# Six places for the copies on their way to DRAM, a cast moved behind the stores, two sums moved past a marker

## The chip, the cores and the metric

The kernel runs on one core of a Trainium2 chip. The metric is the device time of one execution in microseconds (us), the median over runs. A core has a matrix engine (PE, with its weight loads listed as PEld), a vector engine (DVE), a scalar engine (ACT), a general engine (POOL) and a queue engine (SP); SP, POOL and ACT also issue DMA transfers, and 16 DMA engines carry them.

## The reference, cut to what matters

Attention with a sigmoid in place of the softmax, then a feed-forward block with a GELU, all in float32:

```python
# q, k, v: (8, 12, 448, 64); w_in: (768, 2048); w_out: (2048, 768)
scores = scale * np.matmul(q, k.transpose(0, 1, 3, 2)) - np.log(S)
attn = 1.0 / (1.0 + np.exp(-scores))
attn_out = np.matmul(attn, v)                     # (8, 12, 448, 64)
x = attn_out.transpose(0, 2, 1, 3).reshape(3584, 768)
h = x @ w_in
g = 0.5 * h * (1.0 + erf(h * inv_sqrt2))
return g @ w_out
```

## The kernel before, in words

**Two stages.** The attention runs first (0 to 256 us of the trace), then the feed-forward block (256 us to the end, 4032 matmuls without a pause). The attention is cut into 24 **units** of four heads, three units for each of the eight batches. Units 0, 1 and 18 to 23 run alone (`single`); units 2 to 17 run two at a time (`paired`, on u = 2, 4, ..., 16; "pair u" below is units u and u + 1). The order on every engine is the order in which the code is written; there is no scheduler.

**A pair on PE.** Twelve score tiles (L482, each three times two matmuls, 72 in all, since each operand is split into `hi` and `lo`), then the values of unit u in two halves (L518) with a small score tail between them (L502), then the values of unit u + 1 in the same way. Four places in PSUM, named by `perm`, hold score tiles and the products `pav` of the values in turn. The fourth score tile of the next pair takes the place in which `pav` of unit u + 1 lies, so it can start only when that has been copied out.

**Marker.** Between the halves of `values`, DVE copies two columns of `pav` into `mark` (L545, the tile `ones` in the profile). PE starts the second half only after that copy, so whatever stands ahead of it on DVE can hold up PE.

**Out of PSUM.** `park(u, p)` is called twice for a unit, at the end of its values: DVE copies half p of `pav` (448 columns) into a place in SBUF (L572) and POOL issues the store from there to the DRAM tensor `scr_x` (L573). The places come from `piece` (tag `tmp`), a ring of three, so that each copy waits until the store of three copies earlier has landed. For the first two batches (u below 6) the copies go mostly straight to SBUF tiles that stay there.

**Casts and differences.** `high_qk` rounds a loaded q/k tile to `hi`, on POOL or DVE (L439), and `split_qk` lets DVE take `lo` = raw - `hi` (L448). In pair u POOL casts three tiles for the next pair: halves 0 and 1 of unit u + 2 and half 0 of unit u + 3 (`after`; pair 16 has only the first two). Half 1 of unit u + 3, the fourth, is cast by DVE during the next scores.

**Decoder.** Meanwhile the two weight matrices are decoded in steps: `go(3)` gives DVE the operations L179, L187 and L194, and `post` lets it take four sums (L107 to L110) and POOL issue seven stores to `scr_in` (L213). In pair u this is: `go(3)` ahead of the first values, `post` between their halves (`idle1`), `go(3)` between the second values' halves (`idle2`). `STEPS` gives the steps of units 18 to 23: how many ahead of the values, how many behind the marker.

**Queues.** Each engine works strictly in order. POOL's row in a pair of before is: three casts, seven stores of the decoder, two stores of unit u, two stores of unit u + 1.

Of the kernel before, what the change touches and what calls it, by code (L numbers as in the profile page):

```python
# [8 lines left out]
F32 = mybir.dt.float32  # L9
# [6 lines left out]
ALU = mybir.AluOpType  # L16
# [6 lines left out]
def tile_sigmoid_attention_gelu_ffn(  # L23
# [10 lines left out]
    nc = tc.nc  # L34
    B, NPAIR, _, S = q.shape
    NU = NPAIR // 2
    D = HALF
    NF, _, NC, _ = w_in.shape
    NO, _, NFH, _ = w_out.shape
# [4 lines left out]
    HT = S // 2  # L44
# [71 lines left out]
    def piece(name):  # L116
        return sb.tile([P, S], F32, tag="tmp", name=name, bufs=3)
# [162 lines left out]

    dec = Decoder()
    PAIRED = range(2, 18, 2)
    STEPS = {18: (3, 0), 20: (3, 1), 21: (4, 1), 22: (4, 1), 23: (4, 0)}
    wst_all = sb.tile([P, WST * WU], F32, name="wst_all", bufs=1)
    STEPS_IN_ALL = 5 * len(CHUNKS) + 2

# [64 lines left out]
    def rows(j):  # L351
        return slice(j * D, j * D + D)

    def x_tile(tag, name):
        pool, bufs = (sb, 4) if tag == "xs" else (late, 1)
        return pool.tile([P, KC, S], F32R, tag=tag, name=name, bufs=bufs)
# [25 lines left out]
    x0 = {(j, k): x_tile("xs", f"x0_{j}{k}") for j, k in ((1, 0), (0, 0), (0, 1), (1, 1))}  # L382
    h0 = sb.tile([P, KC, S], F32R, tag="h0", name="xh0_p1", bufs=1)
    x6 = sb.tile([P, KC, S], F32, tag="h1", name="x0_p6", bufs=1)

    def attention(at, ps):
        raws, vals, parts, probs, pavs = {}, {}, {}, {}, {}
        total = B * NU
        SINGLE = PAIRED[-1] + 2
# [15 lines left out]
        def vacate(u, p, c):  # L405
            vacant.append(probs.pop((u, p, c)))

        def load(u):
            if u >= total or u in loaded:
                return  # L410
            loaded.add(u)
            b, n = divmod(u, NU)
            raw = at.tile([P, 2, 2, S], F32, tag="qk", name=f"qk{u}", bufs=3)
            for pp in (slice(0, 1), slice(1, 2)) if u == 0 else (slice(0, 2),):
                if u == 0 and pp.start == 1:
                    nc.scalar.activation(one, one, AF.Sigmoid)
                hps = slice(2 * n + pp.start, 2 * n + pp.stop)
                nc.sync.dma_start(raw[:, pp, 0], q[b, hps].rearrange("p r s -> r p s"))
                for j in range(2):
                    src = k[b, hps, rows(j), j].rearrange("p r s -> r p s")  # L420
                    queue = nc.scalar if j == 0 and u == 0 else nc.sync
                    queue.dma_start(raw[rows(j), pp, 1], src)  # L422
            raws[u] = raw

        def load_v(u):
            if u >= total:
                return
            b, n = divmod(u, NU)
            vr = at.tile([P, 2, 2, FULL + 1, D], F32, tag="v", name=f"v{u}", bufs=3)
            for p in range(2):  # L430
                nc.sync.dma_start(vr[:, p], v[b, 2 * n + p])
            vals[u] = vr

        def high_qk(u, p, copy):
            hi, lo = (
                at.tile([P, 2, S], F32R, tag=x, name=f"{x}{u}_{p}", bufs=3) for x in ("hi", "lo")
            )
            parts[u, p] = hi, lo
            copy(hi, raws[u][:, p])  # L439

        def split_qk(u, p):
            if u >= total:
                return
            raw = raws[u][:, p]
            if (u, p) not in parts:
                high_qk(u, p, nc.vector.tensor_copy)
            hi, lo = parts[u, p]
            nc.vector.tensor_tensor(lo, raw, hi, op=ALU.subtract)  # L448
# [62 lines left out]
        def values(u, i, tail, order, meanwhile, idle):  # L511
# [39 lines left out]
            for p in range(2):  # L551
                for c in range(FULL):
                    vacate(u, p, c)

        def park(u, p):
            if u < 0:
                return
            b, n = divmod(u, NU)
            if b < 2:
                j, c = divmod(2 * n + p, KC)  # L560
                for i in range(2):
                    dst = x0[j, i].bitcast(F32)[:, c, b * HT : b * HT + HT]
                    src = pavs[u][:, p, i * HT : i * HT + HT]
                    if (j, i) == (0, 0):
                        x = piece(f"x{u}_{p}")[:, :HT]
                        nc.vector.tensor_copy(x, src)
                        nc.gpsimd.dma_start(dst, x)
                    else:
                        nc.vector.tensor_copy(dst, src)
                return  # L570
            x = piece(f"x{u}_{p}")
            nc.vector.tensor_copy(x, pavs[u][:, p])  # L572
            nc.gpsimd.dma_start(scr_x[:, 2 * n + p, b * S : (b + 1) * S], x)  # L573

        def decode(u, place):
            if u >= total:
                return
            if u == total - 1:
                dec.second = first_sum
            dec.go(STEPS.get(u, (0, 0))[place])  # L580

# [12 lines left out]
        def single(u):  # L594
            for p in range(2):
                for c in range(FULL):
                    scores(u, p, c, perm[(FULL * p + c) % 4])
            if u == 0:
                scores_tail(u, perm[3])
            load(u + 3)  # L600
            if u > 0:
                split_qk(u + 1, 0)
                split_qk(u + 1, 1)
            decode(u, 0)
            if u == SINGLE + 1:
                x01, x11, x00 = (x0[jk].bitcast(F32) for jk in ((0, 1), (1, 1), (0, 0)))
                nc.vector.tensor_tensor(x01, x11, x01, op=ALU.subtract)
                nc.vector.tensor_tensor(x6, x01, x00, op=ALU.add)
            if u == SINGLE + 2:
                lo = x0[0, 0]  # L610
                nc.vector.tensor_tensor(lo, lo.bitcast(F32), h0, op=ALU.subtract)

            def meanwhile():
                if u == 0:
                    split_qk(1, 0)
                    split_qk(1, 1)
                if u + 1 == PAIRED[0]:
                    split_qk(u + 2, 0)
                decode(u, 1)
                if u == total - 1:  # L620
                    W.low_to(3)

            def idle():
                if u == SINGLE + 1:
                    nc.scalar.copy(h0, x0[0, 0].bitcast(F32))
                if u >= total - 4:
                    W.high_to(W.ready + 1)

            order = [0, 1, 2, FULL] if u == 0 else [FULL, 0, 1, 2]
            values(u, perm[2], perm[3], order, meanwhile, idle)  # L630
            for p in range(2):
                park(u, p)
            if u in (total - 3, total - 2):
                W.low_to(u - total + 4)
            load_v(u + 2)
            if u == 0:
                dec.go(1)
            if u in (total - 6, total - 5):
                W.load_to(2 * (u - total + 7))

        def paired(u):
            a, b, c, d = perm
            begun = u > PAIRED[0]
            after = [(u + 2, 0), (u + 2, 1)]
            if u + 2 < SINGLE:
                after.append((u + 3, 0))
            load(u + 3)
            load_v(u + 2)
            tiles = [(w, p, c) for w in (u, u + 1) for p in range(2) for c in range(FULL)]
            for n, at_tile in enumerate(tiles):  # L650
                if n == FULL:
                    high_qk(u + 1, 1, nc.vector.tensor_copy)
                scores(*at_tile, perm[n % 4], evict if n in (3, 7) else sigmoid)
                if n == 3:
                    split_qk(u + 1, 1)
                if n in (8, 11):
                    late_sigmoid(*tiles[{8: 3, 11: 7}[n]])
            for w, p in after:
                high_qk(w, p, nc.gpsimd.tensor_copy)
            split_qk(*after[0])  # L660
            if begun:
                dec.go(3)

            def idle1():
                load(u + 4)
                dec.post()
                if len(after) > 2:
                    split_qk(*after[2])
                dec.begin_next()

            values(u, a, b, [FULL, 1, 2, 0], lambda: None, idle1)
            for p in range(2):
                park(u, p)
            load_v(u + 3)
            split_qk(*after[1])

            def idle2():
                load(u + 5)
                dec.go(3)
                dec.begin_next()  # L680

            values(u + 1, c, d, [0, 1, 2, FULL], lambda: None, idle2)
            for p in range(2):
                park(u + 1, p)

        u = 0
# [355 lines left out]
```

## Time and profile before

| | |
|---|---|
| median of 3 runs | 1023.78 us (1019.7 to 1024.88) |
| profiled execution, its own time | 1024.35 us |
| its span in the trace | 1022.6 us |
| PE busy | 1007.7 us (99%) |
| DVE busy | 724.9 us (71%) |
| ACT busy | 667.5 us (65%) |
| POOL busy | 128.8 us (13%) |
| mean granted clock of PE | 0.997 of full speed |

The busy shares are means over two very different stages. PE counts as busy until the modelled end of a matmul, so a short wait can hide behind the end of the one before it; the length of a stretch that holds the same work each time tells more. The 1.75 us between span and time lie outside the trace, before the first and behind the last instruction.

### The profile page before, as it was taken

Reading aid. Unit: us, or ns where it says so; the run is one execution under the profiler, and the core shown is the slowest. Engines: PE = TensorE matmul, PEld = TensorE weight load, DVE = VectorE, ACT = ScalarE, POOL = GpSimd, SP = SyncE. Lnnn points to the kernel's source line nnn. Section 1 sums busy time; section 2 is a strip of 40 time slices with the busy share of each in tenths; the row PEclk is TensorE's granted clock in tenths of the full one; section 3 lists DMA queues with packets and bytes.
Section 4 is the critical chain, followed back from the end, with each engine's and each line's share of the span. In section 5 each row is a group of like instructions: output and inputs, shape, how many; then the busy total and the mean of one; then the engine's idle time right before and its main releaser. Section 6 shows DMA issues by size and latency. Waiting matters only on the chain.

```text
span 1022.6 us, 16579 instructions
## 1 busy us (share of the span) xinstructions
PE 1007.7 (99%) x6406; PEld 903.8 (88%) x6406; DVE 724.9 (71%) x842; ACT 667.5 (65%) x920; POOL 128.8 (13%) x191
## 2 busy tenths in 40 slices
PE   9999999999999999999999999999999999999998
PEld 5655555455999999999999999999999999999998
DVE  3687887777997998683368877634887674368873
ACT  5786676678897666566666655666656467666652
POOL 0244434232232120010000000100000000000000
PEclk9999999999999999999999999999999999999999
DMA  9988999897998584565344455644444553434441
GB/s 272 269 272 287 323 346 330 294 347 231 315 338 278 171 273 142 153 190 173 110 136 124 123 151 164 215 123 124 128 118 149 149 162 110 124 98 135 136 139 66
DMA packets 83215, 199.17 MB, mean 195 GB/s; under 512 B 9408, under 2 KB 33984, under 8 KB 83136
## 3 DMA queue, kind: packets, MB, share of 16 engines
q1 hardware_dynamic: 69360, 152.24, 48.7%
q0 software_dynamic: 11840, 39.23, 11.1%
q10 hardware_dynamic: 1936, 6.63, 2.0%
q8 instruction: 51, 0.84, 0.3%
q14 instruction: 28, 0.23, 0.1%
HBM read 156.10 MB, written 41.29 MB: 193 GB/s over the span
## 4 chain that ended last, share of the span: by engine, by line
PE 85%; DMA 8%; DVE 2%; POOL 2%; issue 2%; SPq 0%; POOLq 0%; ACT 0%; DVEq 0%
PE pf L704 75%; PE sc L482 5%; PE pav L518 5%; DMA scr_x<-x 4%; DMA qk<-k_dram 3%; POOL scr_in L213 2%; DMA raw<-w_in_dram 1%; DVE lo L448 1%; PE sc_t L502 1%; PE pav L532 0%; DMA qk<-q_dram 0%; DVE x L572 0%; POOL hi L439 0%; SPq L422 0%; DVE hi L439 0%
## 5 line engine op out<-in xcount | busy, mean ns | idle before, releaser
L704 PE MATMUL pf<-op,whl 128*128 128x448 f32 x2016 | 382.1, 353 | 0.0
L704 PEld LDWEIGHTS pf<-op,whl 128*128 128x128 f32 x2016 | 380.9, 189 | 0.5 <-DVE op L741 0.2
L704 PE MATMUL pf<-xh_p,whl 128*128 128x448 f32 x1296 | 353.0, 353 | 0.0
L338 DVE TENSOR_TENSOR whl<-wst_all,whl 128x768 fp32r<-128x768 f32 x224 | 213.7, 955 | 153.7 <-ACT whl L331 153.3
L331 ACT CAST whl<-wst_all 128x768 fp32r<-128x768 f32 x224 | 186.0, 830 | 142.4 <-PE pf L704 124.5
L704 PEld LDWEIGHTS pf<-xh_p,whl 128*128 128x128 f32 x1296 | 244.9, 189 | 1.4 <-issue 0.7
L704 PE MATMUL pf<-xl_p,whl 128*128 128x448 f32 x624 | 219.9, 352 | 0.0
L741 DVE TENSOR_TENSOR op<-g,op 128x896 fp32r<-128x896 f32 x112 | 121.5, 1086 | 0.9 <-ACT op L751 0.9
L704 PEld LDWEIGHTS pf<-xl_p,whl 128*128 128x128 f32 x624 | 117.9, 189 | 0.1
L751 ACT CAST op<-g 128x896 fp32r<-128x896 f32 x112 | 104.8, 936 | 1.7 <-PE pf L704 1.7
L518 PE MATMUL pav<-a_all,v 64*64 64x448 f32 x936 | 104.4, 541 | 0.7 <-DVE ones L545 0.7
L457 ACT ACTIVATE a_all<-sc 128x896 f32<-128x896 f32 x91 | 77.6, 930 | 26.3 <-PE sc L482 26.3
L518 PEld LDWEIGHTS pav<-a_all,v 64*64 64x64 f32 x936 | 37.5, 132 | 50.0 <-issue 38.5
L741 DVE TENSOR_TENSOR g<-g,g 128x896 f32<-128x896 f32 x64 | 69.5, 1086 | 0.0
L738 ACT ACTIVATE g<-tmp 128x448 f32<-128x448 f32 x64 | 40.3, 631 | 38.2 <-DVE tmp L741 38.1
L482 PE MATMUL sc<-lo,hi 64*128 64x448 f32 x276 | 54.6, 380 | 9.8 <-DVE x L572 9.8
L738 ACT ACTIVATE g<-pf 128x448 f32<-128x448 f32 x64 | 34.8, 543 | 39.8 <-PE pf L704 39.7
L363 POOL DMA_DIRECT2D x<-scr_x x24 | 18.0, 806 | 324.8 <-ACT g L848 204.2
L741 DVE TENSOR_TENSOR tmp<-pf,g 128x448 f32<-128x448 f32 x64 | 39.8, 623 | 26.2 <-PE pf L704 16.6
L448 DVE TENSOR_TENSOR lo<-qk,hi 128x896 fp32r<-128x896 f32 x46 | 53.8, 1170 | 5.9 <-POOL hi L439 5.4
L482 PE MATMUL sc<-hi 64*128 64x448 f32 x276 | 51.8, 359 | 0.0
L482 PE MATMUL sc<-hi,lo 64*128 64x448 f32 x276 | 51.7, 359 | 0.0
(85 smaller groups left out, 925.8 us busy)
## 6 DMA issues: line engine op xcount, KB each, us to landing
wst_all<-scr_in SPq DMA_DIRECT2D x112, 384.0 KB, 3.2
wst_all<-scr_out SPq DMA_DIRECT2D x112, 384.0 KB, 3.2
v<-v_dram SPq DMA_DIRECT2D x48, 256.0 KB, 9.6
raw<-w_in_dram SPq DMA_DIRECT2D x16, 767.8 KB, 9.9
out_dram<-tmp SPq DMA_DIRECT2D x47, 224.0 KB, 2.1
qk<-q_dram SPq DMA_DIRECT2D x23, 448.0 KB, 9.2
qk<-k_dram SPq DMA_DIRECT2D x46, 224.0 KB, 9.8
scr_out<-wd POOLq DMA_DIRECT2D x36, 256.0 KB, 5.1
```

The costliest lines, as they stand in the source:

```text
L213: nc.gpsimd.dma_start(scr_in[n // 2][:, n % 2], parts[p])
L331: nc.scalar.copy(hl[:, 0], t)
L338: nc.vector.tensor_tensor(hl[:, 1], t, hl[:, 0], op=ALU.subtract)
L363: queue.dma_start(dst[:, :, a], src[:, :, a])
L448: nc.vector.tensor_tensor(lo, raw, hi, op=ALU.subtract)
L457: nc.scalar.activation(to, sc, AF.Sigmoid, bias=NEG_LOG_S, scale=SCALE)
L482: nc.tensor.matmul(sc[:, j], ks[rows(j), 1, keys], braid(qs[rows(j), 0]) if braided else qs[rows(j), 0], start=n == 0, stop=n == last,)
L518: nc.tensor.matmul(pav[rows(j), p], vals[u][half, p, j, c], a[p][half, j], start=not swap and c == order[0], stop=c == (order[-1], FULL - ...
L704: nc.tensor.matmul(bank, a, braid(m), **flags)
L738: nc.scalar.activation(straight(dst), unbraid(src), AF.Gelu)
L741: nc.vector.tensor_tensor(out, a, b, op=op)
L751: nc.scalar.copy(op[:, 0], src)
```

## The change

Three things are changed.

1. `parked` gives `park` its place. A number n = 2u + p counts the copies. Below unit 18, n mod 6 of 0 to 2 takes a place of the old ring, n mod 6 of 3 to 5 takes one of the three slices of `x6` (the tile `x_p` in the rows), which holds nothing until unit 19. From unit 18 on it is the ring of three alone.
2. In `paired`, the third tile of `after` (half 0 of unit u + 3) is cast by POOL behind the stores of unit u, no longer ahead of the decoder's seven stores; its `lo` is taken by DVE in `idle2`, behind the second marker and ahead of `go(3)`, no longer in `idle1`.
3. In the last units, the sum into `x6` (unit 19) and the difference into `x0[0, 0]` (unit 20) go behind the marker, and of unit 18's three decoder steps one does.

```diff
-    STEPS = {18: (3, 0), 20: (3, 1), 21: (4, 1), 22: (4, 1), 23: (4, 0)}
+    STEPS = {18: (2, 1), 20: (3, 1), 21: (4, 1), 22: (4, 1), 23: (4, 0)}
...
+        def parked(u, p):
+            n = 2 * u + p
+            if u >= SINGLE or n % 6 < 3:
+                return piece(f"x{u}_{p}")
+            return x6[:, n % 3]
+
         def park(u, p):
...
-                        x = piece(f"x{u}_{p}")[:, :HT]
+                        x = parked(u, p)[:, :HT]
...
-            x = piece(f"x{u}_{p}")
+            x = parked(u, p)
...
             decode(u, 0)
+            x01, x11, x00 = (x0[jk].bitcast(F32) for jk in ((0, 1), (1, 1), (0, 0)))
             if u == SINGLE + 1:
-                x01, x11, x00 = (x0[jk].bitcast(F32) for jk in ((0, 1), (1, 1), (0, 0)))
                 nc.vector.tensor_tensor(x01, x11, x01, op=ALU.subtract)
-                nc.vector.tensor_tensor(x6, x01, x00, op=ALU.add)
-            if u == SINGLE + 2:
-                lo = x0[0, 0]
-                nc.vector.tensor_tensor(lo, lo.bitcast(F32), h0, op=ALU.subtract)
 
             def meanwhile():
+                if u == SINGLE + 1:
+                    nc.vector.tensor_tensor(x6, x01, x00, op=ALU.add)
+                if u == SINGLE + 2:
+                    nc.vector.tensor_tensor(x0[0, 0], x00, h0, op=ALU.subtract)
...
-            for w, p in after:
+            for w, p in after[:2]:
                 high_qk(w, p, nc.gpsimd.tensor_copy)
             split_qk(*after[0])
...
             def idle1():
                 load(u + 4)
                 dec.post()
-                if len(after) > 2:
-                    split_qk(*after[2])
                 dec.begin_next()
...
             load_v(u + 3)
+            for w, p in after[2:]:
+                high_qk(w, p, nc.gpsimd.tensor_copy)
             split_qk(*after[1])
 
             def idle2():
                 load(u + 5)
+                for w, p in after[2:]:
+                    split_qk(w, p)
                 dec.go(3)
                 dec.begin_next()
```

On DVE, in pair 6, from the last of the decoder's sums to the cast of the fourth tile, before (`lo_0_948` is the difference of the third tile, `lo_1_945` that of the second, `x_...<-pav` are the copies of `park`):

```order
L110 TENSOR_TENSOR sin_984<-wd_811,sin_984 128x384
L448 TENSOR_TENSOR lo_0_948<-qk_807,hi_0_947 128x896
L572 COPY x_0_1012<-pav_956 128x448
L572 COPY x_1_1015<-pav_956 128x448
L448 TENSOR_TENSOR lo_1_945<-qk_741,hi_1_944 128x896
L545 COPY ones<-pav_1022 128x2
L179 SCALAR_TENSOR_TENSOR wd_1050<-raw_715,me_997 128x768
L187 TENSOR_SCALAR raw_715<-raw_715 128x768
L194 ISA wd_1050<-raw_715,wd_1050 128x1536
L572 COPY x_0_1071<-pav_1022 128x448
L572 COPY x_1_1074<-pav_1022 128x448
L439 CAST hi_1_1104<-qk_807 128x896
```

The same place after the change:

```order
L110 TENSOR_TENSOR sin_981<-wd_811,sin_981 128x384
L578 COPY x_0_1008<-pav_953 128x448
L578 COPY x_1_1011<-pav_953 128x448
L448 TENSOR_TENSOR lo_1_945<-qk_738,hi_1_944 128x896
L545 COPY ones<-pav_1021 128x2
L448 TENSOR_TENSOR lo_0_1018<-qk_806,hi_0_1017 128x896
L179 SCALAR_TENSOR_TENSOR wd_1050<-raw_712,me_993 128x768
L187 TENSOR_SCALAR raw_712<-raw_712 128x768
L194 ISA wd_1050<-raw_712,wd_1050 128x1536
L578 COPY x_0_1071<-pav_1021 128x448
L578 COPY x_p_115<-pav_1021 128x448
L439 CAST hi_1_1103<-qk_806 128x896
```

The third tile's difference has moved from ahead of unit 6's copies to behind the second marker, ahead of the decoder's three operations and of unit 7's copies; the second copy of unit 7 goes into a slice of `x6`.

On POOL, from the last store of pair 6's decoder to the first store of pair 8's, before:

```order
L213 DMA scr_in_89<-sin_984 128x384
L573 DMA scr_x<-x_0_1012 128x448
L573 DMA scr_x<-x_1_1015 128x448
L573 DMA scr_x<-x_0_1071 128x448
L573 DMA scr_x<-x_1_1074 128x448
L439 CAST hi_0_1182<-qk_980 128x896
L439 CAST hi_1_1185<-qk_980 128x896
L439 CAST hi_0_1188<-qk_1046 128x896
L213 DMA scr_in_68<-wd_1050 128x384
```

The same place after the change:

```order
L213 DMA scr_in_89<-sin_981 128x384
L579 DMA scr_x<-x_0_1008 128x448
L579 DMA scr_x<-x_1_1011 128x448
L439 CAST hi_0_1017<-qk_806 128x896
L579 DMA scr_x<-x_0_1071 128x448
L579 DMA scr_x<-x_p_115 128x448
L439 CAST hi_0_1181<-qk_977 128x896
L439 CAST hi_1_1184<-qk_977 128x896
L213 DMA scr_in_68<-wd_1050 128x384
```

The third cast now stands between the two pairs of stores, and the decoder's stores follow the second cast.

## Rows read from the trace of the kernel before

**Rows 1.** Windows by pair, then single; columns: start:end, length, PE busy (instructions), PEclk, DMA share, GB/s.

```profile
26.70:46.45 19.75, 19.64 (x204) 1.00 0.99 261
65.87:85.29 19.42, 19.42 (x205) 1.00 0.92 296
85.29:108.62 23.33, 21.15 (x205) 0.93 0.89 302
108.62:129.89 21.27, 19.52 (x205) 1.00 0.92 318
129.89:150.27 20.38, 19.52 (x205) 1.00 0.93 330
150.27:170.58 20.31, 19.52 (x205) 1.00 0.96 327
170.58:193.99 23.41, 21.14 (x204) 0.93 0.87 298
193.99:206.04 12.05, 10.15 (x105) 1.00 1.04 337
206.04:216.26 10.22, 10.04 (x106) 1.00 1.02 347
216.26:226.88 10.62, 10.09 (x104) 1.00 1.04 367
226.88:236.69 9.81, 9.81 (x104) 1.00 0.60 211
```

**Rows 2.** Waits of PE: who waited for whom, us in total, times, longest.

```profile
PE sc L482 <- DVE x L572: 9.8, 6, 2.3
PE pav L518 <- DVE ones L545: 0.7, 2, 0.5
```

**Rows 3.** Timeline of DVE around pair 6's end: start, length, operation [idle before <-releaser].

```profile
79.52 1.15 DVE L572 COPY x<-pav 128x448 f32<-128x448 f32 x2
80.59 1.08 DVE L448 TENSOR_TENSOR lo<-qk,hi 128x896 fp32r<-128x896 f32 x1
82.42 0.16 DVE L545 COPY ones<-pav 128x2 f32<-128x2 f32 x1 [0.74 <-PE pav L518]
82.60 0.96 DVE L179 SCALAR_TENSOR_TENSOR wd<-raw,me 128x768 uint32<-128x768 uint32 x1
...
84.20 0.96 DVE L194 CUSTOM_DVE_ANT_0 wd<-raw,wd 128x1536 uint16<-128x1536 uint16 x1
85.45 0.62 DVE L572 COPY x<-pav 128x448 f32<-128x448 f32 x1 [0.28 <-PE pav L518]
88.67 0.62 DVE L572 COPY x<-pav 128x448 f32<-128x448 f32 x1 [2.60 <-DMA scr_x<-x]
```

**Rows 4.** The chain that ended last: one store, one load (start, length).

```profile
80.44 8.21 DMA scr_x<-x
...
149.51 10.41 DMA qk<-k_dram
```

**Rows 5.** Timeline of PE: first and fourth score tile of pair 6, fourth of pair 8.

```profile
65.87 0.46 PE L482 MATMUL sc<-lo,hi 64*128 64x448 f32 x2
...
67.68 0.35 PE L482 MATMUL sc<-lo,hi 64*128 64x448 f32 x2
...
89.44 0.46 PE L482 MATMUL sc<-lo,hi 64*128 64x448 f32 x2 [2.18 <-DVE x L572]
```

**Rows 6.** Timeline of POOL in pair 6: two of the casts, the two stores of unit 6.

```profile
69.68 1.66 POOL L439 CAST hi<-qk 128x896 fp32r<-128x896 f32 x1 [8.21 <-PE sc L482]
71.53 0.94 POOL L439 CAST hi<-qk 128x896 fp32r<-128x896 f32 x1 [0.20 <-PE sc L482]
...
80.44 0.54 POOL L573 DMA_DIRECT2D scr_x<-x  x1
82.45 0.54 POOL L573 DMA_DIRECT2D scr_x<-x  x1 [1.47 <-DMA scr_in<-wd]
```

**Rows 7.** Timeline of DVE in unit 20: the difference into `x0[0, 0]`.

```profile
222.79 1.55 DVE L611 TENSOR_TENSOR x<-x,xh_p 128x1344 fp32r<-128x1344 f32 x1
```

## The prediction, made before the changed kernel ran

> **What bounds the kernel now.** I read the lengths of equal stretches first, since PE's busy share hides what matters. A pair of units holds the same PE work each time: 19.42 us in the stretch that begins at 65.87, which has no wait at all, but 19.75, 23.33, 21.27, 20.38, 20.31 and 23.41 us in the others shown [rows 1]. The excess over 19.42 is 0.33 + 3.91 + 1.85 + 0.96 + 0.89 + 3.99 = 11.93 us. The single units behind them take 12.05, 10.22 and 10.62 us against 9.81 in the undisturbed one [rows 1]: 2.24 + 0.41 + 0.81 = 3.46 us. Together 15.4 us of 1024 are lost in the attention; the rest is PE at work, and the change doesn't touch that.
>
> The list of PE's waits says what for: 9.8 us in six waits for DVE's copy out of PSUM, 0.7 us in two waits for the marker [rows 2]. DVE's timeline shows why the copy is late: at 85.45 the first copy of unit 7 runs as soon as PE is done, the second only at 88.67, after 2.60 us of waiting for a store [rows 3]. The chain names that store: issued at 80.44, landed 8.21 us later [rows 4]. With a ring of three, the fourth copy (unit 7, half 1) needs the place of the first (unit 6, half 0), and the two stand only some 9 us apart. PE then begins the fourth score tile at 89.44 [rows 5].
>
> The waits cost more than their length. In the two longest stretches the granted clock is 0.93 on the mean [rows 1]: 7% of 23.33 and of 23.41 us, 1.6 us each, went to a stretch at the lower level (1.2 instead of 2.4 GHz) that follows the wait. The other stretches have 1.00.
>
> **Part 1, six places.** A copy now needs the place of the copy six before it. Stores land in about 8 us [rows 4]; six copies are three units, some 29 us at 19.42 us for two. No copy below unit 18 should find its place taken. It removes the five excesses of the pairs from 85.29 on (11.60 us) and that of unit 18 (2.24 us): 13.84 us, the lost clock included. The places themselves cost nothing: copy and store keep their size, and the slices of `x6` were empty. From unit 18 on the ring of three serves single units; their excess in before is priced under part 3 and holds no store's wait, since the six waits for a copy [rows 2] are the six stretches just summed.
>
> **Part 2, the third cast.** It leaves the decoder's seven stores free to go right behind the second cast, and no longer lets them wait for a load. Its price lies on DVE. The difference `lo`, 1.08 us [rows 3], stood ahead of unit u's copies, where DVE had time (0.74 us idle ahead of the second marker). Now it stands behind that marker, ahead of the decoder's three operations and the copies of unit u + 1, on which PE's fourth score tile waits. I work this out in the times of pair 6, as if no store held it up:
> - Second marker at 82.42, next operation at 82.60 [rows 3].
> - The cast follows unit 6's second store. The copies end at 80.67 (79.52 + 1.15), the store leaves 0.3 us later (as 80.44 after the first copy's end) and takes 0.54 [rows 3, 6], so the cast starts at about 81.5. A cast takes 0.94 us with DVE quiet and 1.66 us at worst [rows 6], so it ends between 82.45 and 83.2. I take 82.6, near the short end, since DVE idles for most of that time.
> - `lo` from 82.7 to 83.7; L179 to L194 as before, 82.60 to 85.16, 2.56 us; two copies, 1.15 us [rows 3]: 87.4. PE restarts 0.15 us behind the copy (89.44 against 88.67 + 0.62 [rows 3, 5]): 87.55.
> - Undisturbed, the fourth tile begins 1.81 us after the first (67.68 - 65.87 [rows 5]), at 85.29 + 1.81 = 87.10.
>
> So a new wait of 0.45 us, and 0.1 us for the restart (of the 13.84 us, 9.8 are waits and 3.2 lost clock; the 0.84 left over six restarts are 0.14 each): 0.55 us. Its ends: 0, if the decoder's operations find time that I don't see, and 1.2 us with the long cast. It falls on every pair with a third tile, pairs 2 to 14, seven of them: 3.9 us (0 to 8). Pair 2 had 0.33 us of excess, which came from the same `lo` in its old place; that goes.
>
> The long cast bears on this: it took 0.72 us more than the one behind it [rows 6], less than one `lo` of 1.08 us, as if it had waited for the rest of one. The Trainium skill ("SBUF — State Buffer", SBUF: two separate sides) says that a DVE operation with two SBUF inputs and a GpSimd operation that reads SBUF exclude each other for a whole instruction, which the 1.66 us agree with. It speaks against the new place: `lo` of the second tile runs until 81.67, so the cast would start then and end at 82.6. By it the sum below is as it stands; by a cast free from 81.5 on it would be 0.1 us less in each of the seven pairs, 0.7 us.
>
> **Part 3, the last units.** In units 19 and 20 an operation of 1.55 us [rows 7] leaves the row ahead of the marker, so the 0.41 and 0.81 us go: 1.22 us. Behind the marker it delays the copies instead. Unit 19 has nothing else there. In unit 20 L179 and L187 follow, together about 2 us; with 1.55 us that is some 3.5 us against the 2.6 us or so until the copies are due, and 0.5 us of that excess is covered by the three score tiles that PE does first. I put 0.2 us (0 to 0.9). The step moved in unit 18 goes into idle DVE time, at nothing; without that cover it would cost its 1 us.
>
> **Sum.** Removed: 13.84 + 0.33 + 1.22 = 15.4 us. New: 3.9 + 0.2 = 4.1 us. Net 11.3 us from the profiled execution's 1024.35: 1013.05 us. The median of the runs is 0.6 us lower, so 1012.5 by it; I say 1013.
>
> **Rivals.**
> *The new wait is hidden.* If the cast is done at the marker and DVE's row closes up by half a microsecond, all 15.4 us are gained: 1009 us. For it: DVE idles 0.28 us ahead of the first copy [rows 3]. Against: 1.0 us is put in.
>
> *Transfers become the limit.* The pairs of 20.38 and 20.31 us ran at 330 and 327 GB/s with a DMA share of 0.93 and 0.96 [rows 1]. The same bytes in 19.42 us would need 343 GB/s, and a share of 1.00. If q/k loads then come late, the casts on POOL wait and with them DVE's row. If the five pairs stay at 20.3 us, 4.5 us are kept, with 1.1 us from pairs 2 and 4 and 0.2: 1014.8 us. Against: the first single units reached shares of 1.02 to 1.04 and 337 to 367 GB/s.
>
> *The places are not free.* Were the three slices held as one tile, each copy would wait for the last store into any of them, and the 9.8 us would stay: 1022 to 1026 us. Against: in the changed program the second copy of unit 7 and both of unit 8 name no store among what they wait for.
>
> *Slower.* POOL's third cast now stands between two pairs of stores, and the second store can itself wait (1.47 us for an older store [rows 6]); or the cast waits for its load, which lands up to 10.41 us after its issue [rows 4]. Then `lo` holds up the decoder's operations, both copies and PE. Each us of delay costs nearly 1 us in each of seven pairs, so at 2.2 us of wait in each the 15.4 us are used up. A delay of 3 us gives 7 x 3.5 = 24.5 us, with two falls of the clock (3.2 us): 1024.35 - 15.4 + 27.7 = 1037 us. Against: the load that landed at 159.92 did so 9.6 us into its pair (begun at 150.27), and the cast is now due 15.6 us into it (81.5 - 65.87); and the older store that the second one waited for now leaves earlier, for the third cast is no longer ahead of it.
>
> **How the numbers follow.** The forecast (1011 to 1016) has 0.53, the hidden wait 0.17, the transfers 0.14, a longer cast or larger waits in the last units (1016 to 1019) 0.07, the places not free 0.05, slower 0.04. The range of 8 in 10 runs from the hidden wait, 1008.5, to 1018, the end with the long cast (8 instead of 3.9 us). A measurement of this kernel can tell about 0.5%, 5.1 us, from no change. Below 1018.7: 0.53 + 0.17 + 0.14 and most of the 0.07, 0.90. Within: 0.06. Slower: 0.04.
>
> **What would show it.** Right: no DVE copy waits for a store below unit 18; pairs of 19.9 to 20.1 us from pair 4 on, with PE's wait of about 0.5 us ahead of the fourth tile released by the copies, and DVE busy without a break from the second marker to them; a clock of 1.00; units 19 and 20 near 9.8 and 10.0 us. Wrong: POOL waiting ahead of the third cast for a load or a store, DVE waiting for POOL behind the marker by more than 0.3 us, or PE waiting at the first marker, where late loads would show.

## The result, and the profile of the changed kernel

The changed kernel takes 1011.49 us (median of four runs, 1010.67 to 1013.38) against 1023.40 us of the kernel before, a ratio of 0.989 (0.986 to 0.992). It is 11.9 us faster. The prediction was 1013.0 us with a range of 1008.5 to 1018. The profiled execution behind the rows below took 1013.38 us, the longest of the four. One execution, of e9, took 1047.01 us at a mean granted clock of 0.949, and the medians and ratios here leave it out.

First the windows by pair and by single unit, as in [rows 1] (start:end, length, PE busy and instructions, PEclk, DMA share, GB/s). The first line is pair 2, the last is unit 21.

```profile
27.25:48.16 20.91, 19.64 (x206) 1.00 1.05 260
48.16:67.92 19.76, 19.51 (x204) 1.00 0.92 285
67.92:87.69 19.77, 19.52 (x204) 1.00 0.92 300
87.69:107.33 19.64, 19.53 (x205) 1.00 1.02 340
107.33:126.95 19.62, 19.51 (x204) 1.00 1.02 352
...
185.86:195.67 9.81, 9.81 (x105) 1.00 1.06 329
195.67:205.48 9.81, 9.81 (x104) 1.00 1.03 397
205.48:215.35 9.87, 9.87 (x104) 1.00 1.05 320
215.35:225.46 10.11, 10.05 (x104) 1.00 0.90 293
```

Pairs 8 to 16 took between 20.31 and 23.41 us in [rows 1]; now all five take 19.62 to 19.64, with a clock of 1.00 in each. Unit 18 went from 12.05 to 9.81, units 19 and 20 from 10.22 and 10.62 to 9.81 and 9.87. But no pair is at 19.42 any more. Pairs 4 and 6, which no store had held up, are 0.34 and 0.35 us longer than that, the later ones 0.20 to 0.22. Over the same twelve stretches, begin of pair 2 to end of unit 21, the kernel before needed 209.99 us and the changed one 198.21: 11.78 us less. The rest of the program is the same but for 0.55 us that this execution lost ahead of pair 2 and 0.23 us behind unit 21; from there on both kernels need some 786 us.

The list of PE's waits, which stood at 9.8 us for the copy [rows 2]:

```profile
PE pav L518 <- DVE ones L545: 1.3, 1, 1.3
...
PE sc L482 <- DVE x L575: 0.5, 2, 0.3
```

The line of 9.8 us is gone. Of waits for copies the list still holds 0.5 us, two waits for the copies into `x0` (L575), at the heads of the windows of pairs 4 and 6; what the later pairs lose is too short to stand in it and shows in the windows. The 1.3 us are one wait for a marker, in pair 2. The chain of work that ended last shows what it came from (start, length):

```profile
23.03 13.67 DMA qk<-k_dram
...
36.86 0.94 POOL hi L439
...
37.82 1.78 DVE lo L448
39.60 0.08 DVE ones L545
```

A load of the program's start took 13.67 us, the cast and the difference followed it, and the first marker of the pair stood behind them. It made pair 2 20.91 us long. In another profile of the same kernel (e8, below) pair 2 took 19.41. A wait at the first marker came with the moved cast (1.26 us here, 0.88 in e5) and without it (0.97 us in e10), so I count it as scatter of the start.

At the second marker of pair 2 it is otherwise. There the old place of the third tile's cast and difference let a late load through to PE: the difference stands ahead of unit 2's copies and of the second tile's difference, and the marker behind them all. In the five profiles without the moved cast DVE was busy right up to that marker, and pair 2 took 19.75, 20.10, 20.41, 19.92 and 21.74 us; in the seven with it DVE stood idle ahead of the marker, and pair 2 took 19.41 or 19.42 us but for the two with a wait at the first marker (20.91 and 20.53). PE behind that marker in e10, without the moved cast, and DVE at it in e8, with it:

```profile
45.77 0.59 PE L518 MATMUL pav<-wst_all,v 64*64 64x448 f32 x1 [0.89 <-DVE ones L545]
```

```profile
43.58 0.16 DVE L545 COPY ones<-pav 128x2 f32<-128x2 f32 x1 [0.71 <-PE pav L518]
```

So the 0.33 us that the kernel before lost there, and PE's waits of 0.16 to 0.89 us there in e1, e3, e4 and e10, are what part 2 spares pair 2: an effect of the change, set off by the scatter of the start.

### The profile page after: what moved, and what is told of

Its sections match the earlier page's. It is cut to its first block, busy times and chain, and to the rows that moved or that the text cites. A ratio compares the mean times of both kernels' runs of the same rounds, so it can differ in the third digit from the quotient of the medians.

```text
span 1011.6 us, 16578 instructions
## 1 busy us (share of the span) xinstructions
PE 1004.6 (99%) x6406; PEld 900.6 (89%) x6406; DVE 723.4 (72%) x842; ACT 666.9 (66%) x920; POOL 129.7 (13%) x191
## 4 chain that ended last, share of the span: by engine, by line
PE 92%; DMA 3%; DVE 3%; issue 1%; ACT 0%; SPq 0%; POOL 0%; DVEq 0%; POOLq 0%
PE pf L712 73%; PE pav L518 10%; PE sc L482 7%; DMA qk<-k_dram 3%; PE sc_t L502 1%; DVE lo L448 1%; DVE tmp L749 1%; PE pav L532 0%; DVE whl L338 0%; DVE wd L179 0%; DVE x L575 0%; DVE wd L194 0%; DVE raw L187 0%; DVE xl_p L749 0%; DVE x L572 0%
```

## The experiments

Four questions had to be settled: which part earns the 11.9 us; whether six places are what is needed; what the 0.2 to 0.35 us per pair are; and what the moved cast does when the places are not there.

**e1, the six places alone.** Part 1 on the kernel before, with its two uses in `park`.

```diff
+        def parked(u, p):
+            n = 2 * u + p
+            if u >= SINGLE or n % 6 < 3:
+                return piece(f"x{u}_{p}")
+            return x6[:, n % 3]
...
-            x = piece(f"x{u}_{p}")
+            x = parked(u, p)
```

> Part 1 alone: the kernel before with six places, everything else in its old order. Theory (the waits for a place make up 13.8 us, lost clock included): about 1009.6 us; every pair from the third on takes 19.42 us, no copy below unit 18 waits for a store, and the excesses of pair 2 (0.33 us) and of units 19 and 20 (0.41 and 0.81 us) stay. Rival (the third cast, which waits for its load ahead of the decoder's stores, holds back the stores and DVE in a denser schedule, so that the places need the moved cast): pairs of 20 us and more, 1013 to 1017 us.

Measured: 1010.64 us (1010.55 to 1010.80), ratio 0.988 (0.986 to 0.990). Its windows from pair 8 to 14 and of units 19 and 20:

```profile
85.52:104.94 19.42, 19.42 (x204) 1.00 1.02 350
104.94:124.36 19.42, 19.42 (x204) 1.00 1.00 338
...
143.78:163.19 19.41, 19.41 (x204) 1.00 1.02 368
...
192.42:202.66 10.24, 10.04 (x106) 1.00 1.04 390
202.66:213.28 10.62, 10.10 (x105) 1.00 1.05 305
```

Every pair from 4 on runs at 19.41 or 19.42 us, PE without a gap. The DMA engines moved up to 368 GB/s at a share of 1.02 meanwhile, so the transfers are not the limit that one rival made of them. Units 19 and 20 keep their old length, as they should without part 3. Part 1 alone earns the whole 11.9 us. Pair 2 was 20.10 us long.

**e2, the moved cast alone.** Part 2 on the kernel before, with its ring of three.

```diff
-            for w, p in after:
+            for w, p in after[:2]:
                 high_qk(w, p, nc.gpsimd.tensor_copy)
...
-                if len(after) > 2:
-                    split_qk(*after[2])
...
+            for w, p in after[2:]:
+                high_qk(w, p, nc.gpsimd.tensor_copy)
             split_qk(*after[1])
...
+                for w, p in after[2:]:
+                    split_qk(w, p)
                 dec.go(3)
```

> Part 2 alone: the kernel before with the third cast behind the stores of unit u and its difference behind the second marker; three places. Theory: no gain, 1022 to 1025 us; the second copy of unit u + 1 still waits for the store of three copies earlier, which leaves no earlier, and the difference's 1.0 us hides in that wait. Rival (the cast was what held the stores back): the waits shrink from 9.8 to under 4 us and the time falls to 1013 to 1017 us.

Measured: 1017.18 us (1016.08 to 1019.56), ratio 0.995 (0.992 to 0.997). My theory gave this part nothing without the places, and it fell: the part earns 5.4 us by itself. The rival came nearer and fell short too: it had 1013 to 1017 us, and waits of under 4 us. Pairs 8 and 14, PE's wait for copies, and POOL and DVE around pair 6's end (start, length, engine, line, operation, idle before):

```profile
85.84:106.26 20.42, 19.51 (x204) 1.00 1.01 333
...
146.26:166.89 20.63, 19.52 (x205) 1.00 0.95 330
```

```profile
PE sc L482 <- DVE x L572: 4.5, 6, 1.4
```

```profile
72.91 1.07 POOL L213 DMA_DIRECT2D scr_in<-wd  x2
...
80.90 1.08 POOL L573 DMA_DIRECT2D scr_x<-x  x2 [0.82 <-DVE x L572]
```

```profile
87.94 0.62 DVE L572 COPY x<-pav 128x448 f32<-128x448 f32 x1 [0.71 <-DMA scr_x<-x]
```

The second copy of unit 7 still waits for the store of unit 6's first, but 0.71 us and not 2.60 [rows 3]. PE's waits for these copies come to 4.5 instead of 9.8 us, the longest is 1.4, and no window of this profile shows a clock below 1.00. The decoder's first two stores leave at 72.91, 6.8 us into the pair. In the kernel before they stood behind the third cast, which waited for its load, and left 10.75 us into it:

```profile
75.23 1.44 POOL L439 CAST hi<-qk 128x896 fp32r<-128x896 f32 x1 [2.76 <-DMA qk<-k_dram]
76.62 1.60 POOL L213 DMA_DIRECT2D scr_in<-wd  x3
```

These last two rows are of the kernel before. With the decoder's stores out earlier, both stores of unit 6 leave together (2 in 1.08 us), where before the second waited 1.47 us for an older store [rows 6]. And the store that the copy needs is 7.02 us under way (in the chain of e2) instead of 8.21 [rows 4]. That is 1.19 of the 1.89 us by which the wait is shorter. The other 0.70 us are no gain: unit 7's first copy itself comes that much later behind unit 6's (86.61 - 79.98 against 85.45 - 79.52), since `lo` now stands ahead of it.

**e7, e2 with the old delay kept.** To see whether the cause is POOL's order or DVE's, a second cast of the same size was put where the third one had stood. It waits for the same load, and nothing reads what it writes.

```diff
             for w, p in after[:2]:
                 high_qk(w, p, nc.gpsimd.tensor_copy)
+            for w, p in after[2:]:
+                nc.gpsimd.tensor_copy(x6[:, :2].bitcast(F32R), raws[w][:, p])
```

> The run with part 2 alone, to which POOL's old delay is given back: at the third cast's old place POOL casts the same tile into a spare tile that nothing reads, which waits for the same load and takes the same time, and the real cast stays behind the stores. Three places. Theory (part 2 alone gained 5 us because the decoder's first stores no longer queue behind a cast that waits for its load, so that they are out of the way when the stores of unit u go): the gain goes, 1021 to 1024 us, waits of PE for the copies back from 4.5 to 8 us or more. Rival (the gain came from DVE, whose difference no longer stands ahead of unit u's copies, so that their stores leave earlier): stays at 1016 to 1019 us.

Measured: 1024.72 us (1019.16 to 1028.41, ten runs), ratio 1.001 (0.999 to 1.003). The 5.4 us are gone. PE's wait for the copies, and the window of pair 16:

```profile
PE sc L482 <- DVE x L572: 8.3, 6, 2.9
```

```profile
169.03:193.06 24.03, 21.15 (x206) 0.93 0.87 290
```

PE is back at 8.3 us of waits, with a mean clock of 0.93 in one pair. DVE's order is that of e2, so the rival, that DVE's order earned the 5.4 us, is out. The gain of e2 came from the decoder's stores that no longer stand behind a third cast on POOL. How much of that is the cast's wait for its load and how much the cast itself, which takes POOL 0.93 us and more, was not separated.

The rows around pair 6 alone would not have shown it (the decoder's stores, and unit 7's second copy):

```profile
76.75 1.73 POOL L213 DMA_DIRECT2D scr_in<-wd  x3
```

```profile
88.39 0.62 DVE L572 COPY x<-pav 128x448 f32<-128x448 f32 x1 [0.59 <-DMA scr_x<-x]
```

The decoder's stores leave late again, 10.11 us into the pair, and yet both stores of unit 6 leave together and the copy waits 0.59 us, no longer than in e2; pair 8 took 20.32 us. That the two stores leave together is thus not what the gain rests on. The waits came back in later pairs. In pair 14, just ahead of the window of 24.03 us, the added cast waits 2.86 us for its load, and unit 15's second copy 1.83 us for a store:

```profile
159.09 1.34 POOL L661 CAST x_p<-qk 128x896 fp32r<-128x896 f32 x1 [2.86 <-DMA qk<-k_dram]
```

```profile
173.11 0.62 DVE L572 COPY x<-pav 128x448 f32<-128x448 f32 x1 [1.83 <-DMA scr_x<-x]
```

The kernel before points the same way: its two pairs with a clock of 0.93 follow pairs 6 and 14, where the third cast waited 2.76 and 2.29 us for its load and the second copy 2.60 and 2.68 us for its store; in pairs 10 and 12, whose third cast waited for no load, the copy waited 1.28 and 1.21. But pair 8, where the cast waited for no load either, had 2.17.

**e3, the last units alone.** Part 3 on the kernel before.

```diff
-    STEPS = {18: (3, 0), 20: (3, 1), 21: (4, 1), 22: (4, 1), 23: (4, 0)}
+    STEPS = {18: (2, 1), 20: (3, 1), 21: (4, 1), 22: (4, 1), 23: (4, 0)}
...
             def meanwhile():
+                if u == SINGLE + 1:
+                    nc.vector.tensor_tensor(x6, x01, x00, op=ALU.add)
+                if u == SINGLE + 2:
+                    nc.vector.tensor_tensor(x0[0, 0], x00, h0, op=ALU.subtract)
```

> Part 3 alone: the two sums behind the marker and one of unit 18's three decoder steps there, on the kernel before. Theory: 1.0 us less in units 19 and 20 (10.22 and 10.62 become 9.8 and 9.8) and 0.33 us more in unit 21, as in the changed kernel; 1022.5 us, within the scatter of the whole time, so the length of the units in the trace decides. Rival (the units are held by something else than the two operations): lengths as before.

Measured: 1020.72 us (1018.62 to 1026.00, ten runs), ratio 0.998 (0.996 to 1.000). The whole time can't tell 1 us from nothing here, since the copies' waits on the ring of three vary from run to run. The windows can: units 19, 20 and 21 take 9.81, 9.87 and 9.91 us, against 10.22, 10.62 and 9.81 [rows 1]. The 0.33 us more that the theory put on unit 21 were 0.10.

**e4 and e10, the first and third part without the moved cast** (the hunks of e1 and e3, run on two chips).

> Parts 1 and 3 without part 2: six places, sums spread, third cast and its difference where they were. Theory: the moved difference is a net cost of 0.2 to 0.35 us in each of seven pairs, so this takes 1.5 us less than the changed kernel: about 1009.5 us, pairs of 19.42 us, pair 2 with its old excess of 0.3 us. Rival (the moved cast lets the denser schedule run): pairs of 20 us or more, PE waiting at the first or second marker, 1012 to 1016 us.

> Parts 1 and 3 without the moved cast, beside the changed kernel on one chip. Theory: pairs of 19.42 us, so 1.5 us less than the changed kernel in a quiet run; but the third cast and its difference wait for a load ahead of unit u's copies, so that a late load reaches PE, and single runs can be 2 to 5 us longer. Rival (no such tie): a scatter as small as that of the run with the places alone, 0.3 us, and 1009 to 1010 us.

Measured: 1011.37 us (1009.75 to 1015.43), ratio 0.989 (0.986 to 0.992), and 1010.09 us (1009.14 to 1012.11), ratio 0.988 (0.985 to 0.990). All pairs from 4 on took 19.41 to 19.43 us in both profiles. Still, the whole time doesn't separate these kernels from the changed one: nine runs with a median of 1010.98 against ten with 1011.38, one inside the other. In e10's profile pair 2 alone lost 2.3 us to late loads (PE waited 1.9 us for two markers). The 1.5 us that the theory gave did not show in e4, and e10 is 1.3 us below e8, on one chip. The moved cast's cost is shown by the windows, 1.7 us over seven pairs (e8, below); against it stands what it spares pair 2. PE's 0.89 us at pair 2's second marker is the late load that the theory of e10 expected; the runs of e10 spread over 3 us, and only the one of 1011.49 us was profiled.

**e5, four places.** The changed kernel with one slice of `x6` in use instead of three.

```diff
-            if u >= SINGLE or n % 6 < 3:
+            if u >= SINGLE or n % 4 < 3:
                 return piece(f"x{u}_{p}")
-            return x6[:, n % 3]
+            return x6[:, 0]
```

> The changed kernel with four places below unit 18 instead of six (one slice of the spare tile beside the ring of three). Theory (a copy waits because the store it needs was issued only some 9 us earlier and takes 8 us and more to land behind other transfers; with four places it is the same copy of the pair before, some 20 us earlier): as the changed kernel, 1010.5 to 1013 us, no copy waiting for a store. Rival (the more places the better, since stores pile up): a part of the 9.8 us of waits comes back, 1014 to 1018 us.

Measured: 1011.72 us (1010.99 to 1012.90), ratio 0.988 (0.985 to 0.992). Pairs from 4 on take 19.61 to 19.77 us as with six places, and no copy waits for a store. One place more than three was all that was missing. With three, a copy needs the place of one that stands some 9 us back; with four, that of a copy two units back, some 19 us, which is beyond the 8 us of a store.

**e6 and e9, one decoder round behind the copies.** The changed kernel with the decoder's third operation (L194) of that row moved behind unit u + 1's copies, to make room for the `lo` that part 2 put there; run on two chips.

```diff
                 for w, p in after[2:]:
                     split_qk(w, p)
-                dec.go(3)
+                dec.go(2)
                 dec.begin_next()
...
             for p in range(2):
                 park(u + 1, p)
+            dec.go(1)
```

> The changed kernel with the third of the decoder's operations in the second gap (0.96 us of DVE) behind the copies of unit u + 1 instead of ahead of them. Theory (the 0.2 to 0.35 us that each pair still loses are DVE's row between second marker and copies being too long): pairs of 19.42 to 19.5 us, 1.5 us less than the changed kernel, about 1010 us, clearest in the trace. Rival (DVE has no time there either, and the operation comes back as a wait at the next pair's first marker or its eighth tile): pairs of 19.6 us and more, no gain.

> The changed kernel with the decoder's third operation of the second gap behind the copies of unit u + 1, beside the changed kernel on one chip. Theory: 1.5 us less than the changed kernel, pairs of 19.42 us in all eight. Rival (the 1.5 us between the medians were the scatter of the start and the first loads): no difference above 0.5 us.

Measured: 1009.95 us (1009.18 to 1010.49), ratio 0.987 (0.984 to 0.990), and on the other chip 1009.28, 1009.57, 1009.86, 1010.09 and 1014.40 us, ratio 0.988 (0.985 to 0.991). Windows of e6 for pairs 6, 8 and 14, and its DVE at pair 6's end:

```profile
65.51:84.93 19.42, 19.42 (x206) 1.00 0.93 310
84.93:104.34 19.41, 19.41 (x204) 1.00 1.00 345
...
143.17:162.59 19.42, 19.42 (x205) 1.00 1.01 353
```

```profile
82.23 1.09 DVE L448 TENSOR_TENSOR lo<-qk,hi 128x896 fp32r<-128x896 f32 x1
...
85.08 0.63 DVE L578 COPY x<-pav 128x448 f32<-128x448 f32 x1 [0.29 <-PE pav L518]
85.62 0.61 DVE L578 COPY x_p<-pav 128x448 f32<-128x448 f32 x1
86.16 0.95 DVE L194 CUSTOM_DVE_ANT_0 wd<-raw,wd 128x1536 uint16<-128x1536 uint16 x1
```

The copies start as soon as PE is done (0.29 us of idle time, released by PE, as in [rows 3]), and all eight pairs are at 19.41 or 19.42. So DVE's row behind the second marker was the cause of what the pairs had above that, and 0.96 us out of it is enough to end it. This is the best version that was run, with the moved cast in it: on the chip of e9 the changed kernel took 1010.79 to 1012.55 us (e8, below).

**e8, the changed kernel again**, on the chip of e7, e9 and e10.

> The changed kernel unaltered, as the base for the two that follow: 1011.5 us, pairs of 19.62 to 19.77 us, no copy waiting for a store.

Measured: 1011.38 us (1010.79 to 1012.55), ratio 0.989 (0.987 to 0.991). Pair 2 19.41 us, pairs 4 and 6 19.76 and 19.74, the others 19.61 to 19.64. With the start undisturbed, the pairs' excess is 1.7 us in all, and e9 against e8 on the same chip (medians 1009.86 and 1011.38) is 1.5 us less.

## Why the prediction was right, point by point

**The bound.** Right. What could be gained was the excess of equal stretches over the undisturbed one, and nothing outside the attention moved.

**Part 1, 13.84 us.** As sized. In e1 the pairs from 8 to 16 are 11.6 us shorter together and unit 18 2.24. The two spells of lower clock went with the waits, in e1 and in the changed kernel. Of the profiled executions, e1's (1010.80) is 13.55 us shorter than that of the kernel before (1024.35); the medians differ by 11.9, since the latter lies 1.8 us above its kernel's median on the chip of e1 (1022.55).

**Part 2's new wait, the term that was mis-sized.** The mechanism was right: `lo` stands behind the second marker, ahead of the decoder's operations and the copies, and PE's fourth score tile is late by it. It was put at 0.55 us in each of seven pairs, 3.9 us; the windows give 0.34 and 0.35 at the ends of pairs 2 and 4 and 0.20 to 0.22 at the other five, 1.76 us. Pairs 2 and 4 end in four copies of 224 columns, straight to SBUF, that take 0.13 us longer than the two of 448 (48.95 to 50.23 against 88.48 to 89.63). DVE at the end of pair 6, the place that the prediction worked out from [rows 3]:

```profile
82.91 1.08 DVE L448 TENSOR_TENSOR lo<-qk,hi 128x896 fp32r<-128x896 f32 x1
84.83 0.16 DVE L545 COPY ones<-pav 128x2 f32<-128x2 f32 x1 [0.83 <-PE pav L518]
85.00 1.09 DVE L448 TENSOR_TENSOR lo<-qk,hi 128x896 fp32r<-128x896 f32 x1
86.01 0.95 DVE L179 SCALAR_TENSOR_TENSOR wd<-raw,me 128x768 uint32<-128x768 uint32 x1
...
87.61 0.96 DVE L194 CUSTOM_DVE_ANT_0 wd<-raw,wd 128x1536 uint16<-128x1536 uint16 x1
88.48 0.62 DVE L578 COPY x<-pav 128x448 f32<-128x448 f32 x1
89.02 0.61 DVE L578 COPY x_p<-pav 128x448 f32<-128x448 f32 x1
```

POOL and PE there:

```profile
82.76 1.07 POOL L579 DMA_DIRECT2D scr_x<-x  x2 [0.83 <-DVE x L578]
83.83 0.96 POOL L439 CAST hi<-qk 128x896 fp32r<-128x896 f32 x1
```

```profile
87.69 0.46 PE L482 MATMUL sc<-lo,hi 64*128 64x448 f32 x2
...
89.78 0.46 PE L482 MATMUL sc<-lo,hi 64*128 64x448 f32 x2
```

The prediction had the cast end 0.18 us behind the marker's start, with ends of 0.03 and 0.78 behind it. It ended 0.04 us before it (84.79 against 84.83) and took 0.96 us, the short end. So `lo` follows the marker at once, and from the marker's start to the copies' end it is 4.80 us (89.63 - 84.83) where 4.98 were forecast. PE restarts 0.15 us behind the copies, as forecast, and begins the fourth tile 2.09 us after the first, 0.28 behind the undisturbed 1.81 [rows 5]; forecast were 0.45. The other 0.1 us, put on top for the restart, was not there at all: the window shows 0.22. Of the 0.33 us that are too much in such a pair, 0.17 are the row from cast to copies, with the cast's end as its largest part (`lo` began 0.17 us behind the marker's start and not 0.28), 0.10 the restart, and 0.06 what the window makes up. A start that is late by 0.28 us does not show the 0.14 us that were left over behind each of the long waits.

The rule that the prediction weighed, from the Trainium skill ("SBUF — State Buffer", SBUF: two separate sides), would let the cast begin only at the end of the second tile's `lo`. That is 83.99 by its row (82.91 + 1.08), and the cast's row begins at 83.83. DVE's rows overlap one another by about 0.08 us too (85.00 + 1.09 against 86.01), so the 0.16 us there neither refute the rule nor bear it out. Elsewhere the same trace agrees with it, in that the two don't run side by side. In pair 4 the third cast and the second tile's `lo` begin together:

```profile
63.29 0.94 POOL L439 CAST hi<-qk 128x896 fp32r<-128x896 f32 x1
```

```profile
63.27 1.92 DVE L448 TENSOR_TENSOR lo<-qk,hi 128x896 fp32r<-128x896 f32 x1
```

`lo` takes 1.92 us instead of 1.08 and ends 0.96 us behind the cast, nearly a whole `lo` later. The sum stood as it was by the rule, and the size of the new wait hangs on the cast's measured end and not on it.

**What the sum left out.** Part 2 was costed as if only its price counted; the prediction names the decoder's stores that go earlier, and puts nothing on them. Without the places they earn 5.4 us (e2, e7). The sum came out right because part 1 takes the same waits: 11.9 us for part 1 alone, 5.4 for part 2 alone, and 11.9, not 17.3, for all three. With the places free, part 2 has nothing left to earn in the pairs behind the second and costs the 1.7 us above.

**Pair 2's 0.33 us.** Right, and for the reason given: with `lo` behind the second marker, DVE is idle ahead of it (19.41 us in e8). In the profiled execution a late load at the first marker put 1.16 us on top of the old length. That PE waits at a first marker was among the signs of being wrong; it showed in pair 2, and it is not an effect of the change (e10).

**Part 3.** Units 19 and 20 gave 1.16 us of the 1.22 forecast. For the copies behind, 0.2 us (0 to 0.9) were put in; unit 21 has 0.30 in this profile and 0.08 in e8. The difference is one operation, L179, 1.43 us here and 1.22 there:

```profile
212.55 1.55 DVE L619 TENSOR_TENSOR x<-x,xh_p 128x1344 fp32r<-128x1344 f32 x1
214.02 1.43 DVE L179 SCALAR_TENSOR_TENSOR wd<-raw,me 128x1024 uint32<-128x1024 uint32 x1
...
216.09 1.15 DVE L578 COPY x<-pav 128x448 f32<-128x448 f32 x2
```

DVE is busy without a break from L619 to the copies, as the prediction said. What made L179 longer in this execution was not tried; e10 has the same 1.43 us, and a unit 21 of 10.10, e1 and e3 to e6 have 1.22 to 1.24.

**The rivals.** *Hidden wait* (1009): not so, e6 shows what it would have been, 1009.95. *Transfers* (1014.8): fell with e1, 368 GB/s at undisturbed length. *Places not free*: fell with the list of waits. *Slower*: its mechanism, POOL's third cast late, did not occur: in pairs 4 to 14 the cast follows the stores at once, as in pair 6 above, and no load holds it up. In pair 2 it waited for its load, a sign of being wrong too, and ended at 43.78, still 1.53 us ahead of the marker.

**The sum.** The terms as measured in the profiled execution are -13.84 + 1.16 + 1.76 - 1.16 + 0.30 = -11.78 us, the 11.78 of the windows. That this execution (1013.38 us) lies so near to the 1013.05 of the sum is in part luck: the new wait was put 2.1 us too high, and pair 2 came out 1.5 us longer than the sum had it. Pair 2 was 1.50 us longer here than in e8, 0.21 us more were lost ahead of it and 0.22 in unit 21, 1.93 of the 2.07 us between the two profiled executions (1013.38 and 1011.31); with an undisturbed start the sum is nearly 2 us too high, and that is the over-sized wait.

## What to carry to other kernels

When a ring of buffers stalls, count how long after a place's last use its next use comes and compare that with the time that its store takes to land: here one place more took the waits away, and three more did no better. Two cures of one wait don't add up; run each alone, and ask of the second what it costs once the first has done the work, and what else it spares (here pair 2's second marker). An operation that is moved into a later row is priced from the fixed event that the row hangs on (here the marker) to the operation that somebody waits for, and if that is late, look for another operation in the row that nobody waits for and put it behind.

## What the runs showed of the hardware that I had not expected

The place in POOL's queue at which other stores leave goes with when a store lands. A 224 KB store of a copy took 6.8 to 8.2 us in the five that the chain of the kernel before holds, 5.7 to 7.5 us in the six of e2, where the decoder's stores had left earlier, and 7.0 to 9.0 us in the four of e7; the kind, the size and the number of the transfers are the same. Whether that is the order of the queue or the load on the DMA engines at that moment was not separated.

A share of DMA engines that reads 1.00 to 1.03 was no sign of a limit: the pairs held 338 to 368 GB/s at their undisturbed length in e1.
